# Block-selected attention with a softplus MLP on one core: one written-out order of 1344 steps is replaced by another

## Chip, core and metric

One core of one Trainium2 chip. The metric is the device time of one execution in microseconds (us); less is better. Engines: TensorE (PE) with its weight loads (PEld), VectorE (DVE), ScalarE (ACT), GpSimd (POOL) and SyncE (SP), which issues most transfers.

## What is computed

The reference, cut to what matters. Attention runs over 4 batches of 8 heads with 768 positions of 64 values:

```python
k_min, k_max = k_chunks.min(3), k_chunks.max(3)
ub = sum(maximum(q * k_min, q * k_max), -1)
ub = where(causal_by_chunk, ub, -1e9)
top_chunks = argsort(ub)[..., -6:]
scores = where(selected & causal, scale * q @ k.T, -1e9)
attn = softmax(scores)
x = (attn @ v) transposed to (3072, 512)
h = x @ w_in
out = (max(h, 0) + log1p(exp(-abs(h)))) @ w_out
```

A chunk is 32 keys, and each query keeps the 6 chunks with the highest bound. w_in is 512 by 2048, w_out 2048 by 512, and softplus stands between them.

## The kernel before, in words

**Units.** A pair is two heads. Batch 0 is cut into eight units: units 0 to 3 are the four pairs with the first half of the queries (3 tiles of 128), units 4 to 7 the same pairs with the second half. Units 8 to 19 are the pairs of batches 1 to 3 with all 6 tiles.

**The order.** The string ORDER holds one word for each step, and the last lines of the kernel call them in that order:

```python
for name, *a in steps_of(ORDER):
    ops[name](*a)
```

Nothing else schedules the work. Each engine takes its own steps in the order of the list and waits, in its own queue, for data and free buffers. A last letter V, A or G says which of DVE, ACT and POOL does the step. The order of the list is so the order of each engine's queue.

**The steps of one unit.** bk, bq, bv (L230) load 128 KB of batch 0 and Lk, Lq, Lv (L251) one pair of a later batch; hk, hq, hv, ck, cq, cr and cv cast to bf16 (L237, L240, L245, L266, L269, L272). kt and qt turn k and q on PE (L295, L302); later batches do it by a transposing transfer (fk, fq, L286). rg reduces k to chunk minima and maxima (L309), pk packs them (L314), kr and qr copy rows (L318, L322), qp and qn split q by sign (L330, L335). U multiplies the bounds (L345), Ua masks them (L352), M finds the 8 highest (L359), T makes the selection rows (L367, L368). In batch 0, a and ac turn and copy these rows (L376, L381); in batch 1 s and sc do it (L387, L391), later a transposing transfer (fs). S is scores (L426), in one to three groups for each head; E the exponential (L432), D the causal mask (L437, on POOL), V the product with v (L453), n the normalization (L463 to L469), X and x the turn to features and its copy (L475, L485), or fx, a transposing transfer.

**The feed-forward steps.** I multiplies x by w_in for half a batch (L495; 4 matmuls of 384 columns in each step), P is softplus (L499). For batch 0, F multiplies by w_out (L507), ob evicts and O stores. For the later batches three levels of a seven-product scheme are used for two token tiles at a time: t mixes weights (L541), g takes differences of tokens (L551), m is one product in two halves (L565), e evicts and adds (L573 to L585), o stores (L589). w issues a weight load from POOL's queue (L594, L597). spin is a matmul of zeros (L197) whose result nobody reads. tE and tP are activations of one row.

**Buffers.** The score tiles S, the products I and the spins share two PSUM buffers (ps_big), and the turns, bounds and outputs of V two others (ps_sm); k and q turns of batch 0 and the results of F and m share the last two (ps_w). Loads and casts have two buffers for each of k, q and v.

## Time and profile before

| | us |
|---|---|
| median of 3 runs | 263.6 |
| lowest, highest | 262.2, 263.87 |
| profiled execution | 263.69 |
| its span, first to last instruction | 262.0 |
| PE busy | 246.1 |
| DVE busy | 183.5 |
| ACT busy | 176.4 |
| POOL busy | 122.5 |

The page of the profile gives one execution. The busy time of an engine is the time in which at least one of its instructions runs. Matmuls overlap, so the mean of one is longer than its share of the busy time. A line of a timeline merges instructions that follow each other; the number behind the x says how many, and brackets hold the idle time of that engine in front of them and what ended it. The granted clock is 1.00 at 2.4 GHz and 0.50 at 1.2 GHz.

### The profile page before, as it was taken

The numbers are of one execution on the slowest core, as the hardware profiler recorded it, in microseconds if no ns is written. First come the engines' busy times: TensorE is split into PE (matmuls) and PEld (weight loads), VectorE is DVE, ScalarE is ACT, GpSimd is POOL, SyncE is SP. The second block draws the span as 40 slices with busy tenths as digits, with TensorE's granted clock in tenths as the row PEclk, the third lists the DMA queues.
The fourth block names the chain that finished last, engine by engine and source line by source line (L and its number), as shares of the span: only waits on it lengthen the run. The fifth ranks groups of instructions, "written<-read, shape, count | busy, mean of one in ns | idle before, by whom it ended". The sixth has DMA issues, their size and how long they took to land.

```text
span 262.0 us, 6544 instructions
## 1 busy us (share of the span) xinstructions
PE 246.1 (94%) x2576; PEld 176.0 (67%) x2576; DVE 183.5 (70%) x553; ACT 176.4 (67%) x236; POOL 122.5 (47%) x148
## 2 busy tenths in 40 slices
...
GB/s 150 219 193 178 223 195 171 134 75 236 184 207 226 163 153 189 194 130 244 216 241 213 182 143 146 234 190 82 161 42 93 83 75 99 80 4 0 80 63 100
DMA packets 119903, 39.23 MB, mean 150 GB/s; under 512 B 113728, under 2 KB 115776, under 8 KB 119872
## 3 DMA queue, kind: packets, MB, share of 16 engines
...
HBM read 27.26 MB, written 6.29 MB: 128 GB/s over the span
## 4 chain that ended last, share of the span: by engine, by line
PE 71%; DVE 12%; ACT 6%; DMA 4%; POOL 3%; issue 2%; SPq 1%; ACTq 0%; POOLq 0%; DVEq 0%
PE hp L495 26%; PE op L565 21%; PE sc L426 11%; PE o_ps L453 6%; DMA qf<-in_q_dram 4%; ACT attnT L432 3%; PE op L507 3%; DVE km L309 2%; DVE m L359 2%; POOL attnT L437 1%; PE spin L197 1%; DVE row L368 1%; ACT Kaug L222 1%; DVE vaug L269 1%; DVE Kaug L318 1%
## 5 line engine op out<-in xcount | busy, mean ns | idle before, releaser
L432 ACT ACTIVATE attnT<-sc 128x1024 bf16<-128x1024 f32 (+3 forms) x96 | 84.1, 917 | 16.0 <-PE sc L426 14.5
L495 PE MATMUL hp<-xT,w_in_sb 128*128 128x384 bf16 x512 | 86.9, 326 | 0.0
L499 ACT ACTIVATE gT<-hp 128x768 bf16<-128x768 f32 x64 | 51.8, 810 | 39.1 <-PE hp L495 39.0
L495 PEld LDWEIGHTS <-w_in_sb 128*128 128x128 bf16 x512 | 49.3, 98 | 31.0 <-issue 0.2
L426 PE MATMUL sc<-Qaug,Kaug 128*128 128x128 bf16 (+3 forms) x400 | 51.9, 259 | 2.6 <-ACT Qaug L381 1.3
L437 POOL TENSOR_SCALAR_AFFINE_SELECT attnT<-attnT 128x768 bf16<-128x768 bf16 (+1 forms) x40 | 31.2, 781 | 26.8 <-ACT attnT L432 24.4
L426 PEld LDWEIGHTS <-Kaug 128*128 128x128 bf16 x400 | 29.9, 99 | 13.4 <-issue 3.8
L565 PEld LDWEIGHTS <-gT 128*128 128x128 bf16 x288 | 27.4, 98 | 5.4 <-DVE ob L579 0.7
L309 DVE TENSOR_REDUCE km<-kT_sb 128x24 bf16<-128x768 bf16 x24 | 22.3, 945 | 10.1 <-DMA kT_sb<-kb 10.1
L565 PE MATMUL op<-w_out_sb,gT 128*128 128x256 f16 x216 | 28.8, 272 | 0.0
L453 PE MATMUL o_ps<-vaug,attnT 128*128 128x65 bf16 x672 | 26.7, 194 | 1.4 <-DVE vaug L269 1.3
L453 PEld LDWEIGHTS <-attnT 128*128 128x128 bf16 x672 | 25.1, 98 | 4.2 <-issue 1.8
L507 PE MATMUL op<-w_out_sb,gT 128*128 128x512 f16 x96 | 26.4, 379 | 0.0
L551 DVE TENSOR_TENSOR mixa<-gT 128x1024 bf16<-128x1024 bf16 x7 | 6.9, 981 | 14.5 <-ACT gT L499 14.4
L359 DVE MAX8 m<-ubm 128x8 f32<-128x8 f32 (+4 forms) x192 | 16.4, 159 | 0.5
L318 POOL COPY Kaug<-kT_sb 64x768 bf16<-64x768 bf16 x17 | 14.4, 855 | 4.2 <-DMA kT_sb<-kb 3.3
L551 POOL TENSOR_TENSOR mixb<-gT,mixa 128x1024 bf16<-128x1024 bf16 x2 | 4.4, 2222 | 24.1 <-DVE mixa L551 24.0
L469 DVE TENSOR_TENSOR on<-o_ps,rr 128x384 bf16<-128x384 f32 x24 | 13.4, 557 | 0.8
L197 PE MATMUL spin<-zeros 128*128 128x512 bf16 x32 | 11.2, 489 | 1.5 <-DVE zeros L194 1.3
L507 PEld LDWEIGHTS <-gT 128*128 128x128 bf16 x96 | 8.4, 98 | 4.5
L352 DVE TENSOR_TENSOR ubm<-ub,causal 128x288 f32<-128x288 f32 (+2 forms) x20 | 7.6, 378 | 3.8 <-PE ub L346 3.3
L314 POOL COPY kmm<-km 64x48 bf16<-64x48 bf16 (+1 forms) x15 | 3.6, 237 | 14.2 <-DVE km L309 13.0
...
## 6 DMA issues: line engine op xcount, KB each, us to landing
out_dram<-ob SPq DMA_DIRECT2D x24, 256.0 KB, 2.5
...
w_out_sb<-in_moe_w_out_dram POOLq DMA_DIRECT2D x2, 1024.0 KB, 11.2
...
```

Of the source, the lines that this page charges most:

```text
L197: PE.matmul(o, state[0]["zeros"][:, 0:128], state[0]["zeros"], start=True, stop=True)
L309: V.tensor_reduce(st["km2"][:, which, :], st["kT"].rearrange("d (c t g) -> d c t g", t=4, g=CH // 4), axis=AX.XY, op=(ALU.max, ALU.min)[wh ...
L318: COPY[eng](Ka(p, e)[D * (1 - e):D * (2 - e), t0 * 128:t1 * 128], st["kT"][e * D:(e + 1) * D, :])
L359: V.max(out=st["m8"][:, t, e, :], in_=st["ubm"][:, t, 0:max(8, 4 * (t0 + t + 1)), e])
L426: PE.matmul(sc[:, o:o + (z - a) * 128], Ka(p, e)[:, tj * 128:(tj + 1) * 128], Qa(p, e)[:, a * 128:z * 128], start=True, stop=True)
L432: A.activation(st["at", e][:, g * 1024:g * 1024 + n], st["sc", e, g][:, 0:n], ACT.Exp, scale=scale)
L437: G.affine_select(out=d, in_=d, compare_op=ALU.is_ge, fill=0.0, base=0, channel_multiplier=-1, pattern=[[0, n], [1, 128]])
L453: PE.matmul(o[:, t, :], st["at", e][:, a:a + 128], va[:, tj, e, :], start=(tj == 0), stop=(tj == t0 + t))
L495: PE.matmul(hps[b, h, s][:, n, 0:HALF], w_in_sb[:, dt, ft * 128:(ft + 1) * 128], xT[b][:, dt, h * HALF:(h + 1) * HALF], start=(dt == 0), s ...
L499: A.activation(gT[b, h][:, 2 * s:2 * s + 2, :], hps.pop((b, h, s))[:, :, 0:HALF], ACT.Softplus)
L507: PE.matmul(held[b, t], g[:, ft, c:c + 128], w_out_sb[:, ft, :], start=(ft == 0), stop=(ft == KFF - 1))
L565: PE.matmul(o, x[:, f], y[:, f], start=(f == 0), stop=(f == KH - 1))
```

## The change

Only ORDER changes. All steps of the old list are in the new one with the same tiles and sizes, but for the spins: 9, 7, 2, 2, 2, 2, 2, 2, 2 and 2 (32) before; 9, 1, 4, 2, 7 and 1 (24) after. 127 steps name another engine than before. The diff is cut to the opening and to the places that the prediction speaks of.

```diff
--- before.py
+++ after.py
@@ ORDER @@
-spin9 ident rm0.V bk0.0.1 augb bk0.0.0 bk0.0.2 hk0.0.V cau0 augm kt0 bk1.0.1 bq0.0.2 bq0.0.1 bq0.0.0 bq0.1.2 ar0.1.A
-ar1.1.A ar3.1.A kt1 kr1.1.A ar1.0.A kr0.1.V ar0.0.V hq0.0.G ar3.0.G bk0.1.0 bk0.1.1 bk0.1.2 kr0.0.V kr1.0.V rg0.0
-rg0.1 rg1.0 bq0.1.0 bq0.1.1 rg1.1 kmm spin7 spin2 pk0.0.V qt0 qn0 pk0.1.A pk1.1.G vones hq0.1.G ar2.0.G pk1.0.V qp0.V
-U0 qt1 qn1 Ua0 M0 hk0.1.A qp1.A T0 kt3 spin2 kr3.0.A qt2 bk1.0.2 bv0.1.1 bk1.0.0 bv0.1.0 bv0.0.2 bq1.0.2 bv0.0.1
-bv0.1.2 bv0.0.0 bq1.0.1 bk1.1.2 bk1.1.0 rm1.G hk1.0.G bq1.0.0 bk1.1.1 bq1.1.2 U1 a0.1 spin2 spin2 rg3.0 rg3.1 qn2
-kr3.1.V ac0.1.A S0.1.0 E0.1.0 a0.0 kt2 Ua1 M1 T1 kr2.1.A ac0.0.A qp2.V D0.1 ar2.1.G w0 a1.1 S0.0.0 a1.0 qt3 rg2.0
-rg2.1 pk2.0.V ac1.1.V qn3 pk3.1.V E0.0.0 pk2.1.V U2 S1.1.0 kr2.0.V Ua2 M2 T2 hv0.0.0.G V0.1 D0.0 hq1.0.G V0.0
-hv0.1.0.A pk3.0.A ac1.0.A qp3.A E1.1.0 U3 S1.0.0 kt5 spin2 n0 Ua3 M3 T3 E1.0.0 a2.1 a2.0 ac2.1.V a3.1 ac2.0.A ac3.1.A
-hv0.0.1.A S2.1.0 a3.0 S2.0.0 E2.1.0 rg5.0 ac3.0.V w1 D1.1 D1.0 V1.1 X0 V1.0 rg5.1 S3.1.0 qt5 x0.V n1 qp5.V hv0.1.1.G
-D2.1 E2.0.0 D2.0 V2.1 S3.0.0 E3.1.0 D3.1 E3.0.0 D3.0 X1 V2.0 spin2 spin2 x1.A kr5.1.V qn5 n2 V3.1 V3.0 X2 n3 pk5.0.V
-kt4 spin2 X3 x3.V x2.A kr5.0.A I0.0.2.1 I0.0.2.0 P0.0.2 pk5.1.G w2 I0.0.3.1 U5 qt4 I0.0.3.0 hk1.1.G P0.0.3 I0.0.1.0
-I0.0.1.1 P0.0.1 qp4.V rg4.0 rg4.1 pk4.0.V qn4 pk4.1.G U4 I0.0.0.1 I0.0.0.0 tP P0.0.0 kr4.0.V kr4.1.V cau1 kt6 kt7 Ua5
...
-bv1.0.0 bv1.1.2 bv1.1.1 P0.0.7 hq1.1.V qt6 M5 kr7.1.V T5 a5.0 ac5.0.V a4.0 S4.1.1 qn6 qp6.V ac4.0.V a5.1 qt7 zs0
...
-V7.0 V7.1 X6 Lk9 fq9 Lk10 n7 F0.0.4 F0.0.5 F0.0.6 X7 fq8 F0.1.7 F0.0.7 ck9.V fk9 pk8.0.V ob0.1.V qr9.0.V qp9.V rg9.1
-rg9.0 qr8.1.V qn8 Lk11 Lq10 x6.A x7.A I0.1.7.0 I0.1.7.1 P0.1.7 I0.1.5.0 I0.1.5.1 P0.1.5 pk8.1.A I0.1.1.1 I0.1.1.0
...
-kr9.0.G qr9.1.G ck11.G pk9.1.G fk10 Lq11 I0.1.2.1 I0.1.2.0 U8 P0.1.2 qr8.0.A Ua8 M8 T8 ob0.0.V I0.1.4.1 U9 I0.1.4.0
-P0.1.4 I0.1.6.0 s8 cq11.G sc8.0.A fk11 Ua9 rg10.0 sc8.1.V M9 T9 rg11.0 rg11.1 Lv11 fq10 qn10 Lv8 fq11 I0.1.6.1 P0.1.6
-tP F0.5.0 F0.5.1 S8.0.0 F0.3.0 S8.1.1 F0.3.1 F0.5.2 F0.3.2 F0.3.3 E8.1.1 E8.0.0 S8.1.2 E8.1.2 F0.3.4 S8.0.2 F0.5.3 s9
...
-S10.0.0 E9.1.2 ob0.3.A Lq13 Lv9 cv9.V D9.1 cq13.G D9.0 t1.1.G Lv10 F0.2.2 S10.0.1 E10.0.0 sc11.0.V V9.1 sc11.1.V
-S11.0.1 F0.4.0 E10.0.1 S11.0.2 V9.0 F0.2.3 E11.0.1 S10.0.2 n9.1 fk13 rg13.0 cr13.V n9.0 E11.0.2 E10.0.2 S10.1.0
...
-g1.1.1.V g2.1.1.V Ua14 M14 T14 rg16.0 e2.1.0 Ua15 M15 cq16.A T15 cr14.G D13.0 g4.1.0.G Lq17 fk17 O0.4 fs14.1 Lv15
...
-e5.1.0 rg17.0 g4.1.1.G g3.1.1.V D12.1 cv14.G D12.0 g1.1.2.V g2.1.2.V S13.1.0 E12.0.1 E13.1.0 D13.1 kr16.0.G m2.1.1.0
...
-g1.3.0.V g2.3.0.V g4.3.0.V g3.3.0.V m1.3.0.0 m1.3.0.1 m2.3.0.0 m2.3.0.1 e1.3.0.A m6.3.0.0 m6.3.0.1 g1.3.2.V e2.3.0
-m5.3.0.0 m5.3.0.1 m7.3.0.0 m7.3.0.1 m3.3.0.0 m3.3.0.1 m4.3.0.0 m4.3.0.1 g2.3.2.V e3.3.0 e4.3.0 e5.3.0 o3.0.0 o3.0.1
-g3.3.2.V g4.3.2.V m2.3.2.0 m2.3.2.1 m6.3.2.0 m6.3.2.1 m5.3.2.0 m5.3.2.1 m7.3.2.0 m7.3.2.1 e2.3.2 e3.3.2 e4.3.2
-m3.3.2.0 m3.3.2.1 e6.3.2 o3.2.0 m4.3.2.0 m4.3.2.1 e7.3.2 o3.2.1
...
+spin9 bk0.0.0 augb augm ar2.0.A kmm bk0.0.2 bk0.0.1 cau0 ident ar1.1.A rm0.V hk0.0.V kt1 rg1.0 rg1.1 bq0.0.1 bq0.0.0
+bk0.1.1 bq0.0.2 pk1.1.G spin1 kt0 ar0.1.G vones kr0.1.V rg0.1 rg0.0 kr0.0.V pk0.0.G bk0.1.0 bk0.1.2 hk0.1.V bk1.1.2
+bq0.1.2 bv0.0.1 bq0.1.0 bv0.0.0 bq0.1.1 kr1.1.A spin4 kr1.0.A hq0.0.A qt1 qp1.A pk0.1.A qt0 qn0 qp0.V U0 qn1 Ua0
+pk1.0.V M0 T0 spin2 kt3 U1 Ua1 M1 rg3.1 rg3.0 a0.1 spin7 a0.0 ac0.0.V hq0.1.G bv0.1.2 bk1.0.0 bv0.0.2 bq1.0.2 bq1.0.0
+bk1.0.1 bq1.0.1 bk1.1.0 bk1.0.2 ac0.1.A kr3.1.A kr3.0.A qt2 kt2 qn2 T1 rg2.1 qp2.V rg2.0 pk2.1.V rm1.V ar0.0.G pk3.1.G
+ar1.0.G bv0.1.0 bv0.1.1 S0.1.0 E0.1.0 a1.1 a1.0 qt3 S0.0.0 ac1.1.A pk2.0.A ac1.0.A kr2.0.A qp3.A E0.0.0 bk1.1.1
+bq1.1.2 bq1.1.0 bq1.1.1 ar2.1.G D0.1 w0 U2 Ua2 M2 T2 hq1.0.V ar3.0.V a2.0 S1.0.0 S1.1.0 w1 pk3.0.G hv0.0.0.G D0.0
+ar3.1.G hv0.0.1.A ac2.0.V qn3 U3 Ua3 M3 T3 V0.0 V0.1 hk1.0.A E1.1.0 kr2.1.V E1.0.0 S2.0.0 a2.1 qt4 ac2.1.A S2.1.0 a3.1
+kt4 E2.0.0 hv0.1.0.G D1.0 D2.0 D1.1 qn4 n0 ac3.1.V rg4.0 V1.0 S3.1.0 a3.0 qp4.A E2.1.0 rg4.1 ac3.0.V V1.1 S3.0.0 V2.0
+n1 pk4.0.A E3.1.0 hv0.1.1.G D2.1 pk4.1.G D3.1 E3.0.0 V2.1 n2 kr4.0.V X0 D3.0 x0.A X1 V3.1 V3.0 x1.A n3 kr4.1.V spin1
+X2 X3 kt5 x2.A U4 qt5 rg5.0 qp5.V kr5.1.V rg5.1 pk5.1.G pk5.0.G w2 cau1 hk1.1.G x3.A I0.0.3.1 I0.0.3.0 P0.0.3 I0.0.1.1
+I0.0.1.0 Ua4 kr5.0.V qn5 P0.0.1 I0.0.0.1 I0.0.0.0 I0.0.2.1 kt7 P0.0.0 I0.0.2.0 kt6 U5 M4 T4 rg7.0 rg7.1 P0.0.2
...
+ac4.1.V T5 kr6.1.V kr6.0.V kr7.1.V a5.0 ac5.0.V a4.0 qt7 qt6 ac4.0.V qn6 qp6.V qn7 qp7.V S4.1.1 a5.1 zs0 w3 U6 S5.0.0
...
+S7.1.0 E7.1.0 D7.1 kr8.1.G Lk9 S7.1.1 n5 t1.1.V rg8.1 E7.1.1 F0.1.4 V6.0 n6 V7.0 F0.1.5 V7.1 X5 F0.1.6 F0.1.7 cq8.A
+x5.A ck9.A tE X6 n7 X7 x6.V x7.V rg8.0 F0.0.6 F0.0.7 Lk10 fq9 fq8 zs1 ck10.V pk8.1.V kr8.0.G ob0.0.V fk9 I0.1.1.0
...
+qn9 rg9.0 qn8 qr9.0.V qr8.1.A rg9.1 I0.1.0.1 I0.1.0.0 U8 P0.1.7 I0.1.4.1 I0.1.4.0 ob0.1.A P0.1.0 Lq10 Lk11 cq10.A
+P0.1.4 I0.1.2.1 I0.1.2.0 pk9.0.V Ua8 M8 T8 ck11.G kr9.0.G fk10 kr10.1.A qp9.A pk9.1.G qr9.1.G rg10.1 Lq11 Lv11 fk11
+Lv8 I0.1.6.1 I0.1.6.0 s8 F0.3.0 F0.3.1 U9 rg10.0 sc8.0.V sc8.1.V P0.1.2 pk10.1.G cq11.G pk10.0.G P0.1.6 kr10.0.V
...
+T11 sc10.0.V n8.0 Lk13 Lk12 Lv10 ck12.V sc10.1.V E9.1.2 E9.1.1 ob0.3.A qr11.1.G ck13.G qr10.1.G Lv9 qr11.0.G D9.1
+S10.0.1 Lq12 S10.0.0 E10.0.1 E10.0.0 cv9.V F0.2.2 s11 F0.4.0 sc11.0.V V9.1 S11.0.2 sc11.1.V n9.1 fk13 Lq13 D9.0 cv10.G
+kr13.0.G F0.2.3 S10.0.2 X8 E11.0.2 S11.0.1 E10.0.2 E11.0.1 V9.0 S10.1.0 F0.2.4 S11.0.0 F0.2.5 t1.0.G rg13.0 n9.0 x8.V
...
+I1.1.4.0 I1.1.4.1 pk12.0.A P1.1.0 ob0.4.A P1.1.4 I1.1.2.0 I1.1.2.1 Lq14 cq14.V Ua13 M13 pk12.1.G T13 t3.0.V P1.1.2
+I1.1.7.1 I1.1.7.0 P1.1.7 I1.0.4.0 I1.0.4.1 P1.0.4 ob0.2.A I1.0.1.0 I1.0.1.1 U12 P1.0.1 I1.0.7.1 I1.0.7.0 P1.0.7
+I1.0.0.1 I1.0.0.0 Lq15 Lk16 cq15.G fq14 fk15 P1.0.0 t4.0.V qn14 t3.1.V Lv15 rg15.1 O0.3 kr15.1.V rg15.0 ck16.V Ua12
+fk14 rg14.0 M12 qp14.V I1.1.3.1 I1.1.3.0 I1.1.5.0 I1.1.5.1 fq15 fs13.1 kr14.0.G rg14.1 kr14.1.G P1.1.3 I1.0.3.0
+I1.0.3.1 P1.1.5 fs13.0 T12 g1.1.0.V P1.0.3 g2.1.0.V g3.1.0.V qn15 pk15.0.G cr15.G Lk17 O0.2 Lv14 fs12.1 fs12.0 fk16
...
+m6.1.0.0 m6.1.0.1 m5.1.0.0 m5.1.0.1 S13.0.2 M14 g4.1.0.V e2.1.0 T15 S12.1.0 m7.1.0.0 m7.1.0.1 E13.0.2 E12.1.0 S12.0.0
+m3.1.0.0 S12.0.2 m3.1.0.1 m4.1.0.0 E12.0.0 E12.0.2 S12.1.1 S12.0.1 m4.1.0.1 V13.0 g2.1.1.V T14 E12.1.1 O0.4 Lk19 Lq17
...
+g4.1.1.V E13.1.0 S13.1.1 m2.1.1.0 m2.1.1.1 V12.1 S14.1.2 m6.1.1.0 pk16.0.V n12.0 rg17.1 pk17.0.V e1.1.1.V g3.1.1.V
...
+I3.1.2.0 I3.1.5.1 I3.1.5.0 P3.1.2 tP o2.2.1 o2.2.0 o3.1.0 o3.1.1 P3.1.5 g1.3.0.V g2.3.0.V g4.3.0.V g1.3.2.V g3.3.0.V
+m1.3.2.0 m1.3.2.1 e1.3.2.A m1.3.0.0 m1.3.0.1 m2.3.0.0 m2.3.0.1 e1.3.0.A m6.3.0.0 m6.3.0.1 m5.3.0.0 e2.3.0 m5.3.0.1
+m7.3.0.0 m7.3.0.1 m3.3.0.0 e3.3.0 m3.3.0.1 m4.3.0.0 g2.3.2.G g3.3.2.G e4.3.0 m2.3.2.0 m4.3.0.1 e5.3.0 o3.0.1 o3.0.0
+m2.3.2.1 m6.3.2.0 m6.3.2.1 m5.3.2.0 m5.3.2.1 e2.3.2 g4.3.2.G m7.3.2.0 m7.3.2.1 e3.3.2 e4.3.2 m3.3.2.0 m3.3.2.1 e6.3.2
+o3.2.0 m4.3.2.0 m4.3.2.1 e7.3.2 o3.2.1
```

## Rows read from the trace of the kernel before

**Rows 1.** Busy time by stage: stretch; length, PE, PEld, DVE, ACT, POOL, clock, DMA, GB/s.

```profile
0.00:30.39 30.39, 22.36 (x215) 13.78 (x215) 21.96 (x90) 18.62 (x33) 17.67 (x38) 0.89 1.01 188
30.39:42.60 12.21, 11.82 (x92) 7.32 (x91) 8.78 (x36) 8.44 (x12) 1.58 (x4) 1.00 1.17 209
42.60:63.40 20.80, 19.91 (x273) 14.15 (x274) 11.54 (x44) 17.92 (x23) 12.71 (x20) 1.00 0.83 137
63.40:74.40 11.00, 10.52 (x86) 6.38 (x85) 8.21 (x28) 8.11 (x11) 4.55 (x6) 1.00 1.34 201
74.40:109.40 35.00, 32.72 (x405) 21.65 (x406) 31.37 (x90) 28.69 (x38) 25.37 (x29) 1.00 1.04 190
109.40:168.30 58.90, 58.90 (x671) 45.21 (x670) 52.00 (x162) 48.84 (x65) 32.19 (x33) 1.00 0.97 193
168.30:250.00 81.70, 81.70 (x772) 60.65 (x771) 42.89 (x95) 45.76 (x59) 28.47 (x20) 1.00 0.39 83
250.00:262.00 12.00, 8.20 (x74) 6.88 (x71) 6.78 (x13) 0.00 (x0) 0.00 (x0) 0.98 0.24 89
```

**Rows 2.** PE's waits: who waited for whom; us in total, times, longest.

```profile
PE o_ps L453 <- DVE vaug L269: 1.3, 1, 1.3
PE sc L426 <- ACT attnT L432: 1.2, 2, 0.7
...
PE qa L376 <- DVE row L368: 0.8, 2, 0.5
...
PE sT L387 <- DVE row L368: 0.5, 1, 0.5
PE x_ps L475 <- ACT xT L485: 0.4, 1, 0.4
```

**Rows 3.** Instruction groups, whole span: busy us, mean ns, idle before and what ended it.

```profile
L197 PE MATMUL spin<-zeros 128*128 128x512 bf16 x32 | 11.2, 489 | 1.5 <-DVE zeros L194 1.3 <-ACT attnT L432 0.2
...
L551 POOL TENSOR_TENSOR mixd<-gT,mixb 128x1024 bf16<-128x1024 bf16 x4 | 8.8, 2198 | 1.5 <-issue 1.5
...
L551 DVE TENSOR_TENSOR mixb<-gT,mixa 128x1024 bf16<-128x1024 bf16 x7 | 5.7, 812 | 0.2
...
L266 DVE CAST qb<-qf 128x768 bf16<-128x768 f32 x5 | 2.8, 559 | 0.9 <-DMA qf<-in_q_dram 0.9
```

**Rows 4.** Timeline of the opening, POOL, PE, ACT and PE again: start, us, what.

```profile
7.79 0.82 POOL L240 CAST row<-qf 128x768 bf16<-128x768 f32 x1 [3.36 <-DMA qf<-in_q_dram]
...
12.95 0.50 PE L376 MATMUL qa<-ident,row 128*128 128x128 bf16 x3 [0.45 <-DVE row L368]
13.25 1.91 PE L197 MATMUL spin<-zeros 128*128 128x512 bf16 x4
...
15.84 0.81 ACT L432 ACTIVATE attnT<-sc 128x768 bf16<-128x768 f32 x1 [1.87 <-PE sc L426]
...
30.23 2.23 PE L495 MATMUL hp<-xT,w_in_sb 128*128 128x384 bf16 x12
```

**Rows 5.** One microsecond of the opening: length, PE busy, clock, DMA, GB/s.

```profile
14.00:15.00 1.00, 1.00 (x4) 0.50 1.27 220
```

**Rows 6.** Timeline around V9.1: POOL, DVE, PE.

```profile
92.29 2.12 POOL L541 TENSOR_TENSOR mixed<-w_out_sb 128x1024 f16<-128x1024 f16 x1
...
92.60 2.23 DVE L269 CAST vaug<-vf 128x768 bf16<-128x768 f32 x1
...
94.88 0.81 PE L453 MATMUL o_ps<-vaug,attnT 128*128 128x65 bf16 x21 [1.29 <-DVE vaug L269]
```

**Rows 7.** Timeline of the end phase: DVE and PE.

```profile
246.68 0.69 DVE L551 TENSOR_TENSOR mixa<-gT 128x1024 bf16<-128x1024 bf16 x1 [2.10 <-ACT gT L499]
...
250.00 1.04 PE L565 MATMUL op<-w_out_sb,gT 128*128 128x256 f16 x8
...
256.12 1.04 PE L565 MATMUL op<-w_out_sb,mixd 128*128 128x256 f16 x8
...
257.52 1.05 PE L565 MATMUL op<-mixed,gT 128*128 128x256 f16 x8 [0.37 <-DVE ob L579]
```

104 lines of the change are left out of this document (48 added, 56 removed).

## Prediction

> **What bounds the kernel now.** I read the busy time by stage first [rows 1]. The stages are cut at the places where the list goes over from attention to the feed-forward products. The reader is to see that TensorE (PE) is busy for all of 109.4 to 250 us, at full clock, and that its idle time is elsewhere: 30.39-22.36 = 8.0 us before the first product, then 0.4, 0.9, 0.5 and 2.3 us in the four stages up to 109.4, and 3.8 us in the last 12. That is 15.9 of 262.0 us. The list of PE's waits [rows 2] says what ended the larger ones behind the opening. Only those pieces can be won by a new order, because every matmul of the old list is in the new one except some spins. The spins stand in the opening and took 11.2 us there [rows 3], in time that PE would mostly have waited through. The end of the kernel is PE work, one last eviction and a store.
>
> The profiled execution took 263.69 us, 1.7 us more than its span of 262.0, and lies 0.1 us above the median of 263.6. I work the sum against 263.69 and take off the 0.1 at the end.
>
> **The change, part by part.** No tile, shape or formula changes. The order of the steps changes, 127 steps go to another engine (33 from POOL to DVE and 27 back, 27 from DVE to ACT and 23 back, 17 between ACT and POOL), and 24 spins stand where 32 stood. The moves are mostly copies and casts, and 17 of them are token differences and weight mixes (11 to DVE, 6 to POOL), which count more: one takes about 2.2 us on POOL and 0.81 on DVE [rows 3]; a cast of one pair takes 0.56 on DVE [rows 3].
>
> *Opening, -0.5 us.* In both lists the q cast that starts everything waits for the seventh load; it ran at 7.79 us and took 0.82 [rows 4]. In the new list ACT does it, so I price that at nothing. The chain behind it is the same (turn, bounds, mask, maximum, select) and ended in a0.1 at 12.95 [rows 4]. DVE now does a k cast in front of it (0.56) and is rid of other steps there; from half a microsecond each way I take -0.5 for a0.1. Behind a0.1 the old list had four spins, 1.91 us, 0.48 each [rows 4], because the granted clock was 0.50 there [rows 5], the 1.2 GHz level, after a stretch in which PE mostly waited. The new list has seven. At 1.2 GHz they take 7 x 0.48 = 3.4 us, at 2.4 GHz half of that, 1.7. Against 1.91 that is +1.5 or -0.2, and it delays a0.0 and the first scores, which stand behind the spins in PE's queue, and with them the first exponential, at 15.84 [rows 4]. In return the new list does U1, the second pair's maximum and both w_in loads earlier, and has one spin behind S0.1.0 where the old list had eight. The path to the first product (30.23, [rows 4]) is a line of eight exponentials with scores, copies and masks between them. With a warm clock I get it 1.3 us earlier, with a cold one 0.3 later; I take the middle, -0.5. What is late next is the two-buffer rotation of the score banks: S2.0.0 needs E1.0.0, and a2.1 now stands behind S2.0.0.
>
> *First product stage (30.4 to 42.6), -0.8 us.* qt4, kt4, qt5, kt5 and U4 now run before the products, in the opening's gaps; the old list had qt4, U4, U5 and two k turns between them. PE loses about a third of a microsecond of work here. I take -0.4. The bounds of units 4 and 5 are then done earlier, so T5 no longer holds up a5.0, which waited 0.4 us of the 0.8 in [rows 2]: -0.4.
>
> *Second stage pair (42.6 to 74.4), -0.7 us.* x6 and x7 go from ACT, where they stood behind a cast, to DVE. The wait of 0.4 us for the x buffer [rows 2] goes, or half of it, if DVE is late with n7: -0.2. U8 stands six half-products (6 x 4 matmuls of 384 columns, about 3.9 us) in front of s8 instead of two and a half. The 0.5 us that s8 waited for its selection [rows 2] goes: -0.5. The score bank's wait for the first exponential behind a change of activation tables (part of the 1.2 in [rows 2]) has four feed-forward parts to cover it as before; -0.1.
>
> *Third stage (74.4 to 109.4), -0.4 us.* The largest single wait is V9.1's, 1.3 us for v [rows 2]. The rows behind it [rows 6]: a weight mix on POOL ran from 92.29 to 94.41; the v cast on DVE began at 92.60 and took 2.23 us instead of 0.56, and V9.1 began when it had ended. In the new list that mix (t1.1) is DVE work some 35 us earlier. Then 1.0 of the 1.3 goes. But t1.0 now stands on POOL beside the casts and range reductions of units 12 and 13. If a cast meets it there, DVE loses up to 1.7 again (2.23-0.56), and a normalization behind it holds a PSUM buffer. From 0 to 1.7 I take +0.6, because the transposes behind n10 have feed-forward parts as cover. On SP's queue Lv9 now stands behind Lk13, Lk12 and Lv10, and it needs the buffer that cv8 frees, now a POOL step; if it lands late, V9.1 waits for the load instead of the cast, which is in the same bounds.
>
> *Fourth stage (109.4 to 168.3), +0.4 us.* DVE is busy for 52.0 of 58.9 us here [rows 1]. The new list gives it three more differences or mixes (3 x 0.81 = 2.4) and six more casts (6 x 0.56 = 3.4); of smaller steps it gets four and gives away eight, at about half a microsecond -2. That is +3.8, so 55.8 of 58.9, and about 2 us more are drawn in from the next stage. POOL loses two differences and with them time in which DVE is held as at 92.60. PE, which had no idle time here, can only lose: 0 if the DVE steps stay in front of their users, up to 3.8 if each of them delays PE. I take +0.4, near the lower end, as DVE still has 3 us left.
>
> *The rest, 0.* From 168.3 to 250 PE is full [rows 1], with DVE at 42.9 of 81.7: moves there hide beside the products. In the end phase three differences go from DVE to POOL (g2, g3 and g4 of the last tile pair). g1 of that pair is now fourth in DVE's queue, so it ends at about 246.68 + 4 x 0.69 = 249.4 [rows 7], and POOL's three take 3 x 2.2 = 6.6, to 256.0. Their last user, m3.3.2, began at 256.12 [rows 7]. Even if it is 0.4 us late nothing is lost, since m4 behind it waited 0.37 us for an eviction anyway.
>
> **Sum.** -0.5 -0.8 -0.8 -0.4 +0.4 +0 = -2.1 on 263.69, so 261.6; less 0.1 for the median, 261.5 us.
>
> One rule of the Trainium skill speaks against the change in the end phase ("SBUF — State Buffer", section "SBUF: two separate sides"): VectorE, when it reads two SBUF inputs or works in a two-port mode, and GpSimd share one port pair, and who starts first holds it for the whole instruction. By that rule g3.3.0 on DVE stands still if g2.3.2 on POOL starts first; the sum would then be the third rival's, below. The cast at 92.60 agrees with the rule.
>
> **Rivals.** *More of the idle time goes.* Clock warm behind a0.1: -1.3 in place of -0.5. No loss on POOL's t1.0 (-0.6) and none in the fourth stage (-0.4). Then -2.1 -1.8 = -3.9: 259.7 us. For it: all waits of [rows 2] have a named cause that the new order moves. Against it: a wait that goes in an in-order queue usually uncovers the next.
>
> *DVE becomes the bound of the fourth stage.* It decides from the point where DVE's steps fill the stage. DVE's 6.9 us of idle time there are waits for PE, ACT and loads; if those waits stay, the 3.8 us come on top, and 1.7 of a cast that meets t1.0 in the third stage too. With the opening cold (+0.3 instead of -0.5) the sum is -2.1 -0.4 +3.8 -0.6 +1.7 +0.8 = +3.2: 266.8 us; with the other two it is slower than before from 0.6 us of stage growth on. For it: 98% is what 55.8 plus the steps drawn in give. Against: fewer POOL steps that hold DVE.
>
> *The end phase holds PE.* g2.3.2 on POOL begins as g1.3.2 ends, at 249.4, just as DVE comes to g3.3.0. If POOL is first, g3.3.0 ends at 249.4+2.2+0.7 = 252.3 and its user, which began at 250.00 [rows 7], comes 2.3 us late, with everything behind it. That gives 261.5+2.3 = 263.8, no change. For it: 1.67 us of such a hold at 92.60. Against: DVE is at the spot already while POOL still has to get its signal.
>
> *The gains are given back.* Opening cold, the waits replaced by others of the same size: -0.3, 263.3 us.
>
> **How the numbers follow.** Forecast 0.45 (260.5 to 262.5 as its own range), more idle gone 0.18, DVE bound 0.14, end phase 0.08, given back 0.15. A measurement of this kernel can tell about 1% from no change, so faster means below 261.0, slower above 266.2. Faster: all of the first rival and 0.4 of the forecast, 0.18+0.18 = 0.36. Slower: half of the DVE case, 0.07. The rest, 0.57, is within 1%. The range takes in the first rival and most of the DVE case: 259.3 to 265.6.
>
> **What would show it.** Right: PE's idle time and spins before 109 us, 12.1+11.2 = 23.3 us now, fall by about 2.5 us, first product at about 29.7, no wait of V9.1 on the v cast, PE still full from the second batch's products to the end phase. Wrong: waits of PE on DVE steps between 109 and 168 us; a granted clock of 0.5 for more than the three short stretches of the old opening; a PE wait on a difference near 250 us. A first product later than 30.4 would make the opening's term wrong, and POOL differences that stretch DVE casts would make the third stage's.

## The result, and the profile after

| | before, same chip | new list |
|---|---|---|
| median, us | 263.2 | 266.94 |
| lowest, highest | 262.2, 263.87 | 265.61, 267.48 |
| profiled execution, its span | 263.69, 262.0 | 266.47, 264.8 |
| mean granted clock | 0.986 | 0.979 |

The ratio of the times is 1.0125 with an interval of 1.0081 to 1.0168: the new list is slower by 0.8 to 1.7%, where 261.5 us was forecast. Medians, here and below, are over all executions; ratios leave out those of over 1.5% above the fastest of the same kernel, and go by the kernel before on the same chip.

The place of the loss is read from the first product (line 495) of each batch in PE's timeline, and from its last matmul. The table has the start of each block and its length to the next one.

| us | to the first product | first half of batch 0 | to batch 1 | batch 1 | batch 2 | batch 3, to PE's end |
|---|---|---|---|---|---|---|
| start before | 0 | 30.23 | 63.39 | 109.40 | 168.11 | 218.29 |
| length before | 30.23 | 33.16 | 46.01 | 58.71 | 50.18 | 40.28 |
| start after | 0 | 32.43 | 64.75 | 108.67 | 170.59 | 221.25 |
| length after | 32.43 | 32.32 | 43.92 | 61.92 | 50.66 | 40.12 |
| difference | +2.20 | -0.84 | -2.09 | +3.21 | +0.48 | -0.16 |

Two of these differences hold moved work. V16.0 and V16.1, 2 x 21 matmuls or some 1.3 us, stand ahead of batch 2's first product in the new list and behind it in the old one, and one half of a product (m4.2.2.1, 4 matmuls) stands ahead of batch 3's. Without these the fourth block lost 1.9 us, the fifth 1.3 and the last 0.3. So the middle of the kernel won 2.9 us, where the prediction had 2.0, and both ends of it lost more.

The busy time by stage of the kernel after, cut at the starts of the table (length, PE, PEld, DVE, ACT, POOL, clock, DMA, GB/s):

```profile
0.00:32.43 32.43, 21.89 (x213) 14.40 (x215) 23.43 (x88) 18.96 (x34) 16.17 (x38) 0.84 1.10 201
32.43:64.75 32.32, 31.53 (x358) 21.19 (x356) 20.01 (x77) 27.34 (x36) 16.15 (x26) 1.00 0.92 148
64.75:108.67 43.92, 42.90 (x489) 28.18 (x488) 39.15 (x121) 37.75 (x49) 25.65 (x31) 1.00 1.10 195
108.67:170.59 61.92, 60.72 (x711) 46.31 (x710) 55.94 (x171) 48.84 (x63) 24.30 (x29) 1.00 1.10 189
```

Beside [rows 1] the reader is to see three things. PE's idle time between the first product and batch 1 is down to 0.8 + 1.0 us. Ahead of the first product PE is idle for 10.5 us, at a lower mean clock (0.84, was 0.89). And in batch 1, where PE never stood still, it now has 1.2 us of idle time while DVE is busy for 55.9 of 61.9 us; the prediction had 55.8 of its stage plus 2 us drawn in.

PE's waits in the kernel after (who waited for whom; us in total, times, longest):

```profile
PE qa L376 <- DVE row L368: 2.8, 3, 2.0
...
PE x_ps L475 <- DVE on L464: 1.2, 2, 0.7
PE ub L346 <- DVE qneg L335: 1.2, 1, 1.2
```

Against [rows 2], V9.1's wait for v, s8's for its row and the one of x_ps for ACT are gone. The wait of qa for its selection row grew from 0.8 to 2.8 us, and those of x_ps and ub for DVE are in the opening too.

The opening in the timeline, ACT and PE:

```profile
11.84 0.50 PE L376 MATMUL qa<-ident,row 128*128 128x128 bf16 x3 [0.52 <-DVE row L368]
...
16.09 0.81 ACT L432 ACTIVATE attnT<-sc 128x768 bf16<-128x768 f32 x1 [1.70 <-PE sc L426]
...
20.12 0.34 PE L376 MATMUL qa<-ident,row 128*128 128x128 bf16 x3 [2.01 <-DVE row L368]
...
22.33 0.20 PE L346 MATMUL ub<-kmm,qneg 128*128 128x24 bf16 x1 [1.19 <-DVE qneg L335]
```

Beside [rows 4], a0.1 came 1.1 us earlier (11.84 against 12.95), but the first exponential 0.25 later (16.09 against 15.84), behind seven spins that took 2.9 us, mostly at 1.2 GHz. Then a2.0 waited 2.0 us and U3 1.2 us for DVE. The last of the eight exponentials on ACT, four in one row before and one after:

```profile
25.11 3.06 ACT L432 ACTIVATE attnT<-sc 128x768 bf16<-128x768 f32 x4
...
29.07 0.81 ACT L432 ACTIVATE attnT<-sc 128x768 bf16<-128x768 f32 x1 [0.27 <-PE o_ps L453]
```

They end at 28.17 and 29.88. So the 2.20 us are 0.25 up to the first exponential, 1.46 in the line of eight (12.33 us before, 13.79 after), and 0.49 from its end to the first product (2.06 and 2.55). That last piece hardly varies: it is 2.06 or 2.07 us in all seven profiles of the old opening and 2.53 to 2.55 in all eleven whose opening ends as the new list's. There kt5, U4 and qt5 stand between the last turn to features and the first product, from 31.94 to 32.43; before, the first product follows that turn at once.

The granted clock in steps of two microseconds (length, PE busy, clock, DMA, GB/s):

```profile
18.00:20.00 2.00, 0.11 (x5) 1.00 1.43 222
20.00:22.00 2.00, 1.02 (x14) 0.95 1.03 178
22.00:24.00 2.00, 1.67 (x25) 0.50 1.11 200
24.00:26.00 2.00, 1.75 (x17) 0.50 1.13 205
26.00:28.00 2.00, 1.89 (x23) 0.50 1.13 205
28.00:30.00 2.00, 1.31 (x20) 0.85 1.12 202
```

Behind these waits the clock was at its lower level, 1.2 GHz, from 22 to 28 us, and each group of five score matmuls there took 0.80 to 0.83 us instead of 0.50. In the profile of before it was 0.50 in 20 to 22 us and back at 1.00 from 24 us on.

PE's waits behind batch 1's first product in the timeline, and POOL in front of the second of them:

```profile
135.95 0.60 PE L426 MATMUL sc<-Qaug,Kaug 128*128 128x128 bf16 x7 [0.47 <-ACT attnT L432]
...
145.08 1.38 POOL L437 TENSOR_SCALAR_AFFINE_SELECT attnT<-attnT 128x768 bf16<-128x768 bf16 x1 [2.16 <-ACT attnT L432]
...
147.24 0.80 PE L453 MATMUL o_ps<-vaug,attnT 128*128 128x65 bf16 x21 [0.52 <-POOL row L272]
...
159.69 0.60 PE L426 MATMUL sc<-Qaug,Kaug 128*128 128x128 bf16 x7 [0.21 <-ACT attnT L432]
...
171.50 0.81 PE L495 MATMUL hp<-xT,w_in_sb 128*128 128x384 bf16 x4 [0.26 <-DMA xT<-on]
```

There was none in this stretch before. The first three are 1.2 us together, all of PE's idle time in batch 1. None of these names a DVE step, though DVE was busy for 29.5 of the 30 us from 130 to 160 (27.2 before).

### The profile page after: what moved, and what is told of

It is laid out like the page before. It is cut to its first block, busy times and chain, and to the rows that moved or that the text cites. A ratio compares the mean times of both kernels' runs of the same rounds, so it can differ in the third digit from the quotient of the medians.

```text
span 264.8 us, 6515 instructions
## 1 busy us (share of the span) xinstructions
PE 247.0 (93%) x2566; PEld 176.1 (67%) x2568; DVE 182.1 (69%) x555; ACT 178.6 (67%) x239; POOL 108.0 (41%) x143
## 4 chain that ended last, share of the span: by engine, by line
PE 58%; DVE 23%; DMA 5%; ACT 4%; issue 4%; POOL 3%; SPq 1%; POOLq 0%; DVEq 0%; ACTq 0%
PE hp L495 20%; PE op L565 14%; PE sc L426 8%; PE o_ps L453 6%; PE op L507 6%; DVE km L309 5%; DMA qf<-in_q_dram 2%; ACT attnT L432 2%; DVE m L359 2%; DVE on L469 1%; DMA kf<-in_k_dram 1%; DMA kT_sb<-kb 1%; DMA out_dram<-ob 1%; DVE qneg L335 1%; PE spin L197 1%
## 5 line engine op out<-in xcount | busy, mean ns | idle before, releaser
L551 DVE TENSOR_TENSOR mixa<-gT 128x1024 bf16<-128x1024 bf16 x7 | 5.9, 842 | 21.6 <-ACT gT L499 21.6
L318 POOL COPY Kaug<-kT_sb 64x768 bf16<-64x768 bf16 x15 | 13.1, 878 | 10.7 <-DMA kT_sb<-kb 10.1
L551 POOL TENSOR_TENSOR gT<-gT 128x1024 bf16<-128x1024 bf16 x3 | 7.3, 2435 | 24.4 <-DVE mixa L551 24.4
L314 POOL COPY kmm<-km 64x48 bf16<-64x48 bf16 (+1 forms) x22 | 5.7, 257 | 23.4 <-DVE km L309 17.6
L577 DVE TENSOR_TENSOR ob<-op,ob 128x512 f32<-128x512 f32 x9 | 6.2, 688 | 7.7 <-PE op L565 7.7
L551 POOL TENSOR_TENSOR mixa<-gT 128x1024 bf16<-128x1024 bf16 x2 | 4.7, 2332 | 16.1 <-DVE gT L551 12.6
```

The source lines that it names most:

```text
L551: TT[eng](s[k], x, y, op=ALU.subtract)
```

## Experiments

All lists hold the same steps, but for spins; only run 9 changes part of the computation, and says which. The diffs show words of the list, cut to the place. "Batch 1" is the fourth block of the table, 58.71 us long before and 61.92 after.

### Where the loss sits: lists put together from both

**1. Old opening, new list behind it.** The old list's words up to its first product, then the new list's remaining ones.

```diff
-spin9 bk0.0.0 augb augm ar2.0.A kmm
...
+spin9 ident rm0.V bk0.0.1 augb
...
 I0.0.3.1 I0.0.3.0 P0.0.3
```

> The old list up to its first feed-forward product, then the new list's remaining steps in the new order. Theory: the new opening costs 2.2 us (first product at 32.43 against 30.23 us), so this is about 2 us faster than the new list, 264.5 to 265, and keeps the loss behind 109 us. Rival: PE catches up with DVE and ACT later whatever the opening does, so an earlier first product is given back in the fourth stage and the time stays at 266 to 267.

Measured: 268.26 us, ratio 1.0181 [1.0148, 1.0215]. A miss. Its first product came at 32.73 us, since the steps that only the new list does early (qt4, U4 and others) fell between the two parts. Batch 1 took 62.98 us. An old opening with this seam says nothing on the opening.

**2. New list up to batch 1, old rest.**

```diff
-I1.1.6.0 I1.1.6.1 qn13 t2.1.V t4.1.V
...
+t2.1.V Lq14 Lv12 fq12 O0.3 Lq15 ck14.A tP t3.1.G cq14.G I1.1.4.1 I1.1.4.0 P1.1.4
...
```

> The new list up to the first product of batch 1, then the old list's remaining steps in the old order and on the old engines. Theory: the new list is 0.7 us ahead at that point (108.67 against 109.40) and loses 2.5 us up to the first product of batch 2 and little more behind it; with the old rest it ends about 0.7 us ahead of the old kernel, 262 to 263. Rival: the loss behind 109 us is the price of work that the new middle leaves undone, so the old rest is late as well, 264 to 266.

Measured: 265.57 us, ratio 1.0095 [1.0063, 1.0127]. The first product came at 30.30 and batch 1 at 106.56, 2.8 us earlier than in the profile of before, and then the old rest took 4.4 us longer than before: from there to PE's end 153.5 us instead of 149.17. The direction is the rival's, and it looked as if the gain had been work left undone. Run 4 tests that.

**3. Old opening, new middle, old rest.** Runs 1 and 2 in one list.

```diff
-spin9 bk0.0.0 augb augm ar2.0.A kmm
...
-I1.1.6.0 I1.1.6.1 qn13 t2.1.V t4.1.V
...
+spin9 ident rm0.V bk0.0.1 augb
...
+t2.1.V Lq14 Lv12 fq12 O0.3 Lq15 ck14.A tP t3.1.G cq14.G I1.1.4.1 I1.1.4.0 P1.1.4
...
```

> Old opening, new list from the first product to the first product of batch 1, then the old rest. Theory: the gain of the new middle alone, 2.2 + 0.7 = 2.9 us, so 260 to 261, faster than both. Rival: the parts depend on each other and the gain is given back behind 109 us, 263.

Measured: 268.36 us, ratio 1.0176 [1.0118, 1.0233], above both windows. The first product came at 31.65 us behind the same seam as in run 1. The same waits behind batch 1's first product as in run 2, at the same steps.

**4. Old list up to batch 1, new rest.**

```diff
-I1.1.4.1 I1.1.4.0 P1.1.4 I1.1.1.1
...
+t1.0.G Lv13 O0.5 kr13.1.A kr12.0.G I1.1.6.0 I1.1.6.1 qn13 t4.1.V
...
```

> The old list up to the first I1 word, then the new list's remaining steps in its order with its engine letters; t2.1, t3.1, ck14 and cq14 are done ahead of I1 here as before, so DVE enters the stage without debt. Theory A (the new list's choice of engines behind I1 loads DVE until PE waits, 9.7 to 9.97 us busy in 10): I1 at 109.4, I1 to the end still 152 to 153.5 against 149.2, time 266.5 to 267.5, with waits of PE between 130 and 165. Theory B (the loss is the price of the work that the new middle leaves undone at I1): I1 to the end 149 to 150, time 263.5 to 264.5, no wait above 0.3 us between 130 and 165.

Measured: 269.72 us, ratio 1.0249 [1.0158, 1.0339]; from batch 1 to the end 155.6 us, above both windows. Two of its waits, 0.95 and 1.48 us at 110 and 113, come from the seam, and one of 1.85 us is for the transfer of batch 2's x. Without the seam's two some 153 us are left, and 151 without the one for x as well, against 149.2. So the new rest is slow with nothing left undone, and work left undone isn't needed to explain it.

### The opening

**5. Eight more spins** in front of a2.0, to fill the wait.

```diff
-hq1.0.V ar3.0.V a2.0 S1.0.0 S1.1.0
+hq1.0.V ar3.0.V spin8 a2.0 S1.0.0 S1.1.0
```

> The new list with eight spins more, in front of a2.0, where PE waits 2.0 us for the selection of unit 2. Theory: the clock falls to 0.50 from 21.9 to 28.7 us because PE stood idle from 17.7 to 20.1 and from 21 to 22.3; with the spins it falls later or not, PE's steps there take half the time and the first product comes 1 to 2 us earlier: 264.5 to 266. Rival: the opening is a chain of DVE and ACT steps and PE's clock is beside it; the first product stays within 0.5 us of 32.4, the time at 266 to 267.

Measured: 266.03 us, ratio 1.0119 [1.0051, 1.0187]. In its profile the clock was 1.00 from 12 to 30 us and the first product came at 30.07, 2.4 us earlier. But the end came only 1.25 us earlier, since PE waited 2.22 us for the transfer of batch 2's x, and the ratio hardly moved. The later profiles show why one such pair decides little: the same opening ran at different clocks. Granted clock from 12 to 30 us, and start of the first product:

| list whose opening it is | clock, first product (us) |
|---|---|
| old, seven profiles | 0.64, 31.28; 0.81, 30.23 and 30.13; 0.93, 28.81; 1.00, 28.45, 28.46 and 28.24 |
| new, seven profiles | 0.73, 32.43 and 32.39; 0.76, 31.40; 0.77, 31.08; 0.81, 30.96; 0.91, 30.30 and 30.15 |

The means are 29.37 and 31.24: the new opening is 1.9 us longer. At the same clock it is 0.8 (at 0.81) to about 1.4 us (at 0.91 to 0.93) longer; the rest is that none of the seven had the clock at 1.00. Run 5, the new opening with eight spins more at a clock of 1.00, had its first product 1.6 to 1.8 us behind the old opening at that clock.

**6. Four engine choices and one order of the opening undone.** rm1, hq1.0 and ar3.0 leave DVE, and a2.0 goes behind the scores.

```diff
-rm1.V
...
-hq1.0.V ar3.0.V a2.0 S1.0.0 S1.1.0
+rm1.G
...
+hq1.0.G ar3.0.A S1.0.0 S1.1.0 a2.0
```

> The new list with its opening's chain mended: rm1 and hq1.0 on POOL and ar3.0 on ACT instead of on DVE in front of the selections, and a2.0 behind S1.0.0 and S1.1.0 in PE's queue. Theory (PE's waits of 2.0 and 1.2 us at 20 and 22 let the granted clock fall to 0.50 from 22 to 28): first product at 30.2 to 30.8 instead of 32.4, clock 0.98 or more, time 265.0 to 266.0 if the later stages give part of it back as they did with eight more spins. Rival (the clock falls by itself at some run, whatever the waits): first product at 32 or later, time 266.5 to 267.5.

Measured: 265.96 us, ratio 1.012 [1.0026, 1.0214]. The wait of 2.0 us is gone, but others stand in its place (0.87, 0.70, 0.60), and at a clock of 0.82 the first product came at 31.37, no earlier than in the new list at that clock. The time lies in the theory's window, but not for its reason. That the cause is in these steps is not shown.

**7. The first scores ahead of two turns.**

```diff
-bk1.0.2 ac0.1.A kr3.1.A kr3.0.A qt2 kt2
+bk1.0.2 ac0.1.A S0.1.0 kr3.1.A kr3.0.A E0.1.0 qt2 kt2
```

> The new list with one move in the opening: S0.1.0 stands in front of qt2 and kt2 in PE's queue, and its exponential in front of qt2's users. In the profiles of the new list S0.1.0 comes behind kt2, which waits 0.4 us for a PSUM buffer, and the first exponential begins at 15.2 at full clock against 14.3 in the old list; the last one ends 1.4 us later. Theory (the opening's loss is the line of exponentials that starts late): first exponential 0.5 to 0.9 us earlier at the same granted clock (14.4 to 14.7 at full clock), first product 0.5 to 1 us earlier, time 266.0 to 266.5. Rival (the loss lies behind, in the selections on DVE): first exponential earlier, first product within 0.3 us of the new list's at the same clock, time 266.7 to 267.3.

Measured: 267.08 us, ratio 1.014 [1.0068, 1.0212]. The first exponential came 0.27 us earlier at the same clock (15.82 at 0.72, 16.09 at 0.73), the first product 0.3 us later. The rival holds. Of the 0.8 to 1.4 us by which the new opening is longer at the same clock, 0.49 is the work behind its last exponential; what makes the line of exponentials longer stays open.

### Behind batch 1's first product

**8. The old list's engines in the new order**, from batch 1 on (57 words).

```diff
-ck15.V rg12.1 qn12 ck14.V
...
-U14 cv15.V cv14.V Ua14 ck17.V
...
+ck15.G rg12.1 qn12 ck14.A
...
+U14 cv15.G cv14.G Ua14 ck17.A
...
```

> The new list in its order, but behind the first I1 word every step that has a choice goes to the engine that the old list gave it (57 steps differ, the casts of the later sets among them: DVE takes 6 casts fewer). Theory A (DVE's load behind I1 is the cause): DVE's busy time in 130 to 160 falls from 9.8 to about 9.2 of 10, I1 to the end falls by 1.5 to 3 us, time 264 to 265.5. Rival (it is the order of the list, in which the old letters fit no better): 266.5 to 268.5, with new waits of PE on POOL or ACT instead.

Measured: 274.97 us, ratio 1.0431 [1.0346, 1.0516], far above both windows and the slowest of all: the old engines don't fit the new order. It doesn't tell what DVE's load alone does.

**9. DVE made lighter.** Four additions into the output cover 64 of 256 columns; the rest of these sums is left out.

```diff
-            V.tensor_tensor(o[:, 1:3], held[b, i, 3], o[:, 1:3], op=ALU.add)
+            V.tensor_tensor(o[:, 1:3, 0:64], held[b, i, 3][:, :, 0:64], o[:, 1:3, 0:64], op=ALU.add)
...
```

> The new list unchanged; four of the seven additions with which DVE takes a pair's products into the output tile cover 64 of 256 columns (the rest of those sums is left out of the output). That takes some 0.9 us off DVE for each of the nine pairs, 2.7 us of them between I1 and I2, and touches no other engine. Theory A (DVE's load behind I1 is what holds PE): I1 to I2 falls from 61.9 to 60.5 or less, DVE's busy time in 130 to 160 falls from 9.8 to about 9.0 of 10, time 264.5 to 265.7. Rival (PE waits there on POOL and ACT queues in the order of the list, DVE is merely busy): I1 to I2 61.3 or more, the waits at 136 and 147 stay, time 266.2 to 267.5.

Measured: 265.89 us, ratio 1.0075 [1.0036, 1.0115]. The time fell by about 1 us, into neither window of the two theories as a whole; but batch 1 took 63.14 us, longer than the 61.92 of the new list, with a wait of 1.5 us at 135.16. DVE was busy for 29.0 of 30 us from 130 to 160, but 1.6 us of that is one cast that took 2.17 us instead of 0.55 (below), and in batch 2 PE waited 2.37 us for x.

**10. Three casts on POOL instead of DVE.**

```diff
-U14 cv15.V cv14.V Ua14 ck17.V
+U14 cv15.G cv14.G Ua14 ck17.G
```

> The new list; cv14, cv15 and ck17 on POOL instead of DVE, where POOL has 3.5 us idle in front of its difference at 131.5. DVE is relieved of 1.66 us just ahead of 136. Theory A (DVE's load): I1 to I2 1 us shorter than 61.9, time 265.3 to 266.2. Rival (POOL's queue is what counts): the difference on POOL and the diagonal masks behind it come 1 to 2 us later, I1 to I2 unchanged or longer, time 266.5 to 268.

Measured: 266.36 us, ratio 1.0075 [1.0037, 1.0113]; batch 1 62.79 us, no shorter in its profile, with a wait of 1.59 us for ACT at 160.75. The time is between the two windows. Runs 9 and 10 speak against the theory that DVE's load alone holds PE, but not more than that: the ratio fell by 0.5% in both, and the intervals overlap with the new list's.

**What the profiles have in common.** Set side by side, the profiles differ in single DVE steps that take up to ten times their usual length. In run 2 (new list up to batch 1, old rest), POOL, DVE and PE:

```profile
132.41 2.12 POOL L551 TENSOR_TENSOR mixd<-gT,mixb 128x1024 bf16<-128x1024 bf16 x1
...
132.44 2.16 DVE L367 TENSOR_TENSOR row<-m,minus 128x12 bf16<-128x12 f32 x1
...
136.44 1.03 PE L565 MATMUL op<-w_out_sb,mixd 128*128 128x256 f16 x8 [1.12 <-DVE ob L575]
...
137.61 2.12 POOL L551 TENSOR_TENSOR mixd<-gT,mixb 128x1024 bf16<-128x1024 bf16 x1 [3.08 <-issue]
...
137.82 1.99 DVE L367 TENSOR_TENSOR row<-m,minus 128x12 bf16<-128x12 f32 x1
...
141.24 0.60 PE L565 MATMUL op<-w_out_sb,gT 128*128 128x256 f16 x4 [1.28 <-DVE ob L579]
```

The same steps in the kernel before:

```profile
134.69 0.46 DVE L367 TENSOR_TENSOR row<-m,minus 128x12 bf16<-128x12 f32 x1
...
135.06 2.41 POOL L551 TENSOR_TENSOR mixd<-gT,mixb 128x1024 bf16<-128x1024 bf16 x1
...
138.37 0.21 DVE L367 TENSOR_TENSOR row<-m,minus 128x12 bf16<-128x12 f32 x1
...
138.98 2.12 POOL L551 TENSOR_TENSOR mixd<-gT,mixb 128x1024 bf16<-128x1024 bf16 x1 [1.51 <-issue]
...
139.54 0.42 DVE L579 TENSOR_TENSOR ob<-op,ob 128x256 f32<-128x256 f32 x1
...
140.11 0.56 DVE L469 TENSOR_TENSOR on<-o_ps,rr 128x384 bf16<-128x384 f32 x1
```

A selection step of twelve columns (line 367) takes 0.21 us when it is alone. In run 2 it began 0.03 us behind the start of POOL's difference and ended when that ended, 2.1 us later. In the kernel before it began 0.37 us ahead of the difference and went through. The second one went through ahead of its difference. In run 2 the evictions of lines 575 and 579, further on in DVE's queue, came later for it, and PE had no free bank. It is the stretching of the cast in [rows 6], now on a step that the selection and the evictions stand behind.

The Trainium skill says so ("SBUF — State Buffer", section "SBUF: two separate sides"): VectorE in a two-port mode, or with two SBUF inputs against a GpSimd step that reads SBUF, and GpSimd hold one port pair in turn, each for its whole instruction. The traces agree: the held steps of line 367 have two SBUF inputs, 2.16 us behind 2.12 us, while lines 579 and 469, whose first input is in PSUM, took 0.42 and 0.56 us inside the difference at 138.98. In all twenty traces no cast and no step with two SBUF inputs that began inside a difference or a weight mix of POOL ended before it, while some 290 evictions, normalizations, masks of bounds, maxima and reductions, with one SBUF input at most, did. That a plain cast can work in such a two-port mode is what the Trainium skill says ("SBUF — State Buffer", section "Who interferes with whom"); the traces show only that casts are held, in [rows 6] and in runs 1, 4, 6 and 9.

In the new list's own batch 1 it is the difference g1.1.1 on POOL that meets a cast of DVE. In the profile of the first section the two begin in the same hundredth of a microsecond, and POOL is the one that stands still, 2.54 us instead of 2.12:

```profile
131.54 2.54 POOL L551 TENSOR_TENSOR mixa<-gT 128x1024 bf16<-128x1024 bf16 x1 [3.50 <-ACT gT L499]
131.54 0.55 DVE L266 CAST kb<-kf 128x768 bf16<-128x768 f32 x1
```

In run 6 DVE is the one, POOL, DVE and PE:

```profile
130.27 2.12 POOL L551 TENSOR_TENSOR mixa<-gT 128x1024 bf16<-128x1024 bf16 x1 [1.63 <-ACT gT L499]
...
130.43 2.38 DVE L269 CAST vaug<-vf 128x768 bf16<-128x768 f32 x1 [0.51 <-DMA vf<-in_v_dram]
...
135.41 1.03 PE L565 MATMUL op<-mixed,mixa 128*128 128x256 f16 x8 [1.96 <-DVE ob L573]
```

Length of batch 1 in the profiles whose POOL differences there are those of the one or the other list (run 4 with its seam and run 8 left out):

| rest of the list | no step held over 1 us | a step held |
|---|---|---|
| old | 58.71, 59.32, 59.62, 59.77 | 62.37, 63.06, 63.17 |
| new (runs 9 and 10 among them) | 61.92, 61.17, 62.79, 60.91 | 62.98, 62.83, 63.14 |

With a hold the old rest is 3.5 us longer and the new one 1.3 us, mean against mean of three or four profiles. Two of the three held profiles of the old rest stand behind the new middle and have two waits of 0.5 us more; the third, run 15, is 3.0 us longer. Without a hold the new rest is 2.3 us longer than the old one, of which 1.3 are V16.0 and V16.1: 1.0 us. The profile of the first section had no DVE step held; it is the 61.92, with small waits only. So the hold is no part of the +1.9 us that its table shows. Nor does every hold cost time: in batch 2 of the kernel before, DVE steps at 199.09 and 208.25 took 1.55 and 1.93 us instead of 0.69 beside POOL's differences, and PE was busy for all of that block.

**11. Run 2 with both differences on DVE.**

```diff
-g4.1.0.G
...
-g4.1.1.G
+g4.1.0.V
...
+g4.1.1.V
```

> The run with the new list up to I1 and the old rest, with one thing changed: the two differences g4.1.0 and g4.1.1 (mixd) on DVE instead of POOL. Theory H (in that run the two DVE steps of the selection, 0.21 us as a rule, took 2.16 and 1.99 us because each began inside a difference of 2.12 us on POOL and was held until it ended; DVE's evictions behind them came late and PE waited 1.28 and 1.45 us): no selection step of line 367 over 1 us between 128 and 146, both waits gone, I1 to the end some 2.5 to 3 us shorter than its 153.5, time 262.5 to 263.5. Rival (DVE is simply full there): 0.7 us more on DVE for each, the waits stay or grow, time 265.5 to 267.

Measured: 264.24 us, ratio 1.0035 [1.0008, 1.0061], clear of run 2's interval and between the two windows. The steps of line 367 take 0.22 and 0.21 us again and both waits are gone; in their place is one wait for the difference itself, which now stands behind other DVE work:

```profile
132.42 0.22 DVE L367 TENSOR_TENSOR row<-m,minus 128x12 bf16<-128x12 f32 x1
...
135.85 0.21 DVE L367 TENSOR_TENSOR row<-m,minus 128x12 bf16<-128x12 f32 x1
136.31 0.68 DVE L551 TENSOR_TENSOR mixd<-gT,mixb 128x1024 bf16<-128x1024 bf16 x1
...
137.05 1.05 PE L565 MATMUL op<-w_out_sb,mixd 128*128 128x256 f16 x8 [1.86 <-DVE mixd L551]
```

From batch 1 to the end it took 151.4 us, 2.1 less than run 2. The hold is shown to be the cause of run 2's waits; that a place on DVE is free of charge is not.

**12. The new list with g1.1.1 on DVE.**

```diff
-P1.0.5 g1.1.1.G U15
+P1.0.5 g1.1.1.V U15
```

> The new list with one step changed: the difference g1.1.1 (mixa) on DVE instead of POOL. Theory H (where a cast of DVE begins inside this POOL difference it is held for 1.6 to 1.9 us and PE waits 1.5 to 2 us at 135; that is so in three of the six profiles of the new middle and this fourth stage, and not in the first one taken): no DVE step held over 1 us between 128 and 140, no wait of 1.5 us at 135, I1 to I2 61 to 62, median 0.5 to 1 us under the new list's 266.9, so 265.8 to 266.5. Rival (the hold takes no part in the median): 266.7 to 267.5.

Measured: 265.46 us, ratio 1.0074 [1.0044, 1.0103]. No DVE step is held there and batch 1 took 61.89 us. The ratio is 0.5% below the new list's, 1.3 us, a little more than expected, though the two intervals overlap; run 13 gives the same once more. That the hold makes the difference is not shown. Of the 1.5 us between the two profiles, 1.35 lie ahead of the first product (31.08 and 32.43 us), and batch 1 is as long in both. Run 10, which takes the very casts off DVE that this difference holds, came to the same ratio, but so did run 9, whose profile has a hold.

**13. Runs 7 and 12 in one.**

```diff
-bk1.0.2 ac0.1.A kr3.1.A kr3.0.A qt2 kt2
...
-P1.0.5 g1.1.1.G U15
+bk1.0.2 ac0.1.A S0.1.0 kr3.1.A kr3.0.A E0.1.0 qt2 kt2
...
+P1.0.5 g1.1.1.V U15
```

> The new list with both single moves, S0.1.0 in front of qt2 and kt2, and the difference g1.1.1 on DVE. If the two effects add: 0.5 to 1 us less than the run with g1.1.1 alone (265.46), 264.5 to 265.0. If the fourth stage gives the opening's gain back: 265.3 to 266.

Measured: 265.47 us, ratio 1.0068 [1.0037, 1.0098]. Nothing is added by the opening's step, as run 7 said. Waits of 0.32, 0.52 and 0.47 us stay in batch 1 and at batch 2's x.

### One step of the new list in the old one

**14. t1.1, x6 and x7 on DVE.**

```diff
-E7.1.1 D7.1 cq8.A
+E7.1.1 D7.1 t1.1.V cq8.A
...
-x6.A x7.A
+x6.V x7.V
...
-D9.0 t1.1.G Lv10
+D9.0 Lv10
```

> The old list with three steps taken from the new one: t1.1 on DVE behind D7.1 instead of on POOL in front of V9.1, and x6 and x7 on DVE instead of ACT. If a saving of the third stage is kept: I1 at 107.8 to 108.4 instead of 109.4 with the wait of 1.29 us at 94.88 gone, end 1 us earlier, time 262.2 to 263.0. Rival (what is gained ahead of I1 is given back behind it, as with the new list): I1 at 108, end unchanged, time 263.5 to 264.5.

Measured: 269.24 us, ratio 1.021 [1.0145, 1.0275]. Batch 1's first product came at 113.81 us, through one wait on PE:

```profile
68.34 6.85 PE L495 MATMUL hp<-xT,w_in_sb 128*128 128x384 bf16 x30 [6.44 <-DVE xT L485]
```

In the old list's place x6 and x7 stand on DVE behind a cast and reductions that wait for transfers, which on ACT they did not. The new list has them in front of these.

**15. t1.1 on DVE, x6 and x7 on DVE right behind X7.**

```diff
-E7.1.1 D7.1 cq8.A
...
-X7 fq8 F0.1.7
...
-Lq10 x6.A x7.A I0.1.7.0
...
-D9.0 t1.1.G Lv10
+E7.1.1 D7.1 t1.1.V cq8.A
...
+X7 x6.V x7.V fq8 F0.1.7
...
+Lq10 I0.1.7.0
...
+D9.0 Lv10
```

> As the run with t1.1 alone, and x6 and x7 on DVE right behind X7, that is in front of the casts and row copies that wait for transfers (in the earlier run they stood behind these). If the 6.4 us wait at I0.1 came from what was queued in front of x6 and x7: no wait above 1 us between 60 and 70, I1 at 107.5 to 108.3 where the first product is at 30.2, time 261.8 to 262.8. Rival (t1.1 early on DVE is itself what delayed them): a wait of over 3 us at I0.1 again, time 266 or more, and in the run with t1.1 alone too.

Measured: 263.07 us, ratio 0.9939 [0.99, 0.9977], 0.3 us above the window. The long wait is gone, so it came from the queue in front of x6 and x7. In its profile both selection steps were held in batch 1 (2.05 and 1.98 us; batch 1 took 62.37 us); that execution, 266.74 us, was the longest of the ten.

**16. t1.1 alone**, twice (four runs, then eight).

```diff
-E7.1.1 D7.1 cq8.A
+E7.1.1 D7.1 t1.1.V cq8.A
...
-D9.0 t1.1.G Lv10
+D9.0 Lv10
```

> The old list with one step changed: t1.1 on DVE behind D7.1 instead of on POOL in front of V9.1; x6 and x7 stay on ACT. If a saving of the third stage is kept to the end: no wait at 95, I0.1 to I1 44.6 to 45.0 us instead of 46.0, I1 to the end 149.2, time 262.3 to 263.0. Rival (given back behind I1): I0.1 to I1 44.8, I1 to the end 150.3, time 263.5 to 264.3.

> The run with t1.1 alone again, for a narrower interval beside the one above. Theory (the saving of 1.2 us in the third stage is kept): ratio to before 0.990 to 0.996. Rival (the 1.0 per cent of its first four runs was luck): 0.997 to 1.002.

Measured: 262.49 us, ratio 0.9897 [0.9827, 0.9966], and 261.55 us, ratio 0.9929 [0.9901, 0.9957]. It beats both kernels. The way to batch 1 took 44.2 and 44.5 us instead of 46.01, and V9.1, 94.88 in [rows 6], no longer waits; its v cast took its usual time (second profile, DVE and PE):

```profile
90.32 0.56 DVE L269 CAST vaug<-vf 128x768 bf16<-128x768 f32 x1
...
92.94 0.80 PE L453 MATMUL o_ps<-vaug,attnT 128*128 128x65 bf16 x21
```

About 1 us of that came back in batch 1 (59.6 and 59.8 us, with one wait of 0.75 and 0.89 us for ACT), and the rest was kept.

**17. t1.1 on DVE as in run 16, and both differences g4 too.**

```diff
-g4.1.0.G
...
-g4.1.1.G
+g4.1.0.V
...
+g4.1.1.V
```

> The old list with t1.1 early on DVE, and g4.1.0 and g4.1.1 on DVE as well. Theory H (the old list loses some 2.9 us in those of its runs in which the two selection steps fall inside POOL's differences, and saves 1.2 us at 95 by the early t1.1): 260.5 to 262.0, and less spread than the run with t1.1 alone. Rival (DVE, 9.3 of 10 busy there, becomes the bound with 1.4 us more): 262.5 to 264, with waits of PE on DVE between 136 and 150.

Measured: 263.76 us, ratio 1.002 [0.9991, 1.005]. The rival's time. No step is held in batch 1 of its profile, but PE waits 1.86 us for the difference on DVE as in run 11. Its twelve times lie closer together (262.66 to 265.4) than those of run 16 (260.6 to 266.41 and 260.89 to 265.69): I read this as a dependable wait in place of an occasional one, but neither profile of run 16 has a step held in batch 1, so the occasional one is not shown.

## Why the prediction was wrong

**The opening, -0.5, was +2.2** (+1.9 in the mean of seven profiles each). This is the first step that failed, and it failed behind the first exponential. The parts up to there nearly cancelled, as with the cold clock they were to: a0.1 came 1.1 us earlier instead of 0.5, and the seven spins took 2.9 us instead of 1.91, so the first exponential came 0.25 later. But I took the path behind it, "a line of eight exponentials", as unchanged, and looked only at the score buffers. It grew by 1.46 us: a2.0 waited 2.0 us and U3 1.2 us for DVE, and the clock was at 1.2 GHz for six microseconds. The last 0.49 us are kt5, U4 and qt5, which the prediction had "in the opening's gaps" and which stand on the path, between the last turn and the first product. The prediction's own sign for this, a first product later than 30.4, is what the profile shows. That the clock is part of it is seen among profiles of one opening, where a lower clock goes with a later first product; that the waits made it fall is not shown, as run 6 took the longest away and at the same clock gained nothing.

**The middle, -0.8 -0.8 -0.4, was -2.9.** The mechanisms were right and the sizes too small: T5, s8, x6 and x7 and V9.1 stopped waiting, and the early t1.1 alone is worth 1.2 to 1.8 us up to batch 1 (runs 16 and 17), where 1.0 was taken. The +0.6 for t1.0 beside the casts was the wrong part: no cast was held, the one in front of V9.1 took 0.56 us at 93.28.

**The fourth stage, +0.4, was +1.9.** This is the second step that failed. The measured 1.9 lies within its bounds, 0 to 3.8, but the reason for the low end ("DVE still has 3 us left") was not right: where PE's waits stand, DVE was busy for 29.5 of 30 us, and what came late was ACT's and POOL's work. In the profile the loss is three waits of 0.2 to 0.5 us on ACT and POOL, 1.2 us, with PE's restarts behind them; why these steps came late stays open. The rival that makes DVE the bound has the right sign and 266.8 us, close to the 266.94 measured. That closeness is luck: it has the opening at +0.3 where 2.2 came, a stretched cast that didn't come, and the whole of 3.8 us on DVE, while lighter DVE work (runs 9 and 10) left batch 1 as long as it was. In other executions a hold comes on top: profiles with a DVE step held beside a two-input step of POOL are 1.3 us longer in the new rest and 3.0 to 3.5 us in the old one. The prediction had read this hold from one row of the trace, [rows 6], and priced it at two places, t1.0 and the end phase; it did not go through the other POOL differences, among them g1.1.1, which the change itself put on POOL.

**The rest, 0, was about +1.6.** "Moves there hide beside the products" was wrong for the fifth block: PE waited for batch 2's x at 171.50 and stood still among the products of the bounds at 186 us, by an estimate from the starts of these rows 0.9 us together; 0.4 of the 1.3 us can't be placed. The wait for x is the one that varies most: 0.26 us here, 1.85, 2.22 and 2.37 us in the profiles of runs 4, 5 and 9, and none in runs 1, 8 and 10 or in any profile of the old rest. The prediction didn't look at this transfer, and no run changed it.

**The end phase, 0, was right.** The last wait, for an eviction, is 0.37 us as in [rows 7], and the rival that let POOL hold DVE there did not come.

Three slips in its working change nothing: the second stage is headed -0.7 where its terms give -0.8, which the sum uses; s8 stood three half-products behind U8, not two and a half; and the last rival's -0.3 isn't worked out.

**What stays open:** why the line of exponentials is longer in the new opening at the same clock, what made ACT and POOL late in batch 1, why a kernel's opening has the clock at 0.64 in one execution and 1.00 in another, and how many of the unprofiled executions had a step held.
